# Moving loads and stores between the issue queues of SyncE, ScalarE and GpSimd in a fused attention and two-MLP kernel

## The chip, the core and the metric

The kernel runs on one core of one Trainium2 chip. The metric is the device time of one execution in microseconds (us), the median of several runs. The core's engines are TensorE (PE, with its weight loads as PEld), VectorE (DVE), ScalarE (ACT), GpSimd (POOL) and SyncE (SP). Each of SP, ACT and GpSimd can issue DMAs, each in the order of its own instructions, and each waits for semaphores before an issue; an ACT or GpSimd that waits to issue a DMA does no arithmetic meanwhile.

## The reference

Attention over chunks of 32 queries, each with 16 positions of left and 8 of right context and 8 memory positions; its output is the input x of a gated MLP, whose output is the input of a second MLP. All in float32.

```python
# q, k, v: (4, 8, 768, 64), mem_k, mem_v: (4, 8, 8, 64)
for c in range(nc):                                  # 24 chunks of 32
    k_full = concat([mem_k, k[:, :, l_start:r_end]])
    v_full = concat([mem_v, v[:, :, l_start:r_end]])
    a = softmax(scale * q_c @ k_full.T)
    out[:, :, c_start:c_end] = a @ v_full
x = out.transpose(0, 2, 1, 3).reshape(3072, 512)
y = (sigmoid(x @ w_gate) * (x @ w_val)) @ w_out      # 512 -> 1536 -> 512
h = y @ w2_in                                        # 512 -> 2048
result = (h * sigmoid(1.702 * h)) @ w2_out           # 2048 -> 512
```

## The kernel before

**Tiles and blocks.** The 3072 tokens are 32 attention tiles of 96 queries (three chunks), eight to a sequence, and six MLP blocks of 512 tokens. Tiles 0 to 5 are done in a prologue, 6 to 8 beside the first weights; tiles 9 to 31 are the late tiles, in the order 9 to 15, 30, 31, 16 to 29. Every float32 matmul is three matmuls of high and low parts.

**A late tile** (`attention` with `pe_path` False, L390). Its queries (12 DMAs) and keys (16 to 20 DMAs for two tiles) are loaded by SP (helper `dma`, issue at L350), turned by DVE (L532, L540) and multiplied on PE in one burst of 48 small matmuls (L555). The softmax runs on DVE, ACT and GpSimd, the probabilities are turned by DVE (L670), and 16 matmuls with the values (L704) run right ahead of the score burst of a later tile. The values `vn` (L676, `load_ctx`, L405: one DMA for the rows of v, one for the memory rows, one more for a tile at an edge of a sequence) have one buffer for all tiles, so a tile's load waits until the older tile's value matmuls are done. In `load_ctx` the flag `act` chooses ACT's queue; the late tiles set it.

**Where a tile's output goes** (`evict`, L720). For blocks 0 to 3 ACT and DVE cut it into high and low parts (L758, L761), the operands of the first MLP. For blocks 4 and 5 ACT copies it into `qt` (L733), the tile that a later L532 writes, and a DMA by ACT's queue (L735 to L741) stores it to `x_dram`.

**The MLPs.** Blocks 0 to 3 go through the first MLP directly (L821, L828 and L1020); its outputs are stored to `y_dram` by ACT's queue (L1044). Blocks 4 and 5 go through it in a Strassen-like form with seven products of half-sized operands (`part_product`, L1318), and so do the three pairs of blocks in the second MLP. `x_prep` (L1187) makes the operands for a pair: eight loads of 256 KB (issue at L1194, by SP) from `x_dram` or `y_dram` into the buffers `ys0` to `ys3`, differences on DVE (L1200), high and low cuts on ACT (L1178) and DVE (L1182). It is called for blocks 4 and 5 from `x_dram` (L1495), for the first pair from `y_dram` at the start of the second MLP (L1563), and for each next pair while the pair before is worked on (L1866). In the second MLP's second layer (L1655) the weights come from `wo_dram` by SP (L1611), each fetch waiting for its buffer; the weights of the products come from `wc_dram` by SP (L1225).

**The order.** A planner (`Schedule`, L34) gets every operation with an engine, a cost, what it reads and writes, and sometimes a due time. It passes due times back from users to producers, taking 2.0 us and the transfer for an SP operation and 0.2 us for one on another engine, and then fills the engines' queues in simulated time, the earliest due first among the operations that are ready. The queues' order is then fixed. A DMA costs SP or ACT 0.45 us there (0.62 for the key loads), GpSimd 1.0. Score bursts get due times of their own, 150 + 12.6 n (L601), and are held 4.5 us behind their data.

Of the kernel before, what the change touches and what calls it, by code (L numbers as in the profile page):

```python
# [18 lines left out]
P = 128  # L19
# [126 lines left out]
def kernel(  # L146
# [14 lines left out]
    nc = tc.nc  # L161
# [15 lines left out]
    BLK = 512  # L177
# [212 lines left out]
    def attention(t, bufs, banks, pe_path, extra=None, nth=0, last=False):  # L390
# [236 lines left out]
        if pe_path:  # L627

            def ev_norm(c):
                r = (c * CH, (c + 1) * CH)  # L630
                eng = nc.vector if en[c] == "dve" else nc.gpsimd
                norm(eng, T["pw"][r[0] : r[1], :, c * CH : c * CH + CTX], r, (0, CTX))

            def ev_norm_m():
                norm(nc.vector if en[0] == "dve" else nc.gpsimd, T["pw"][:, :, TK:P], (0, TQ), (CTX, KW))

            en = ["pool", "pool", "pool"] if t in (0, 2) else ["dve", "pool", "pool"]
            for c in range(NCK):
                tadd(en[c], 0.75 if en[c] == "dve" else 1.2, lambda c=c: ev_norm(c), r=ke + [kk["sm"]], w=[(kk["pw"], c)])
            tadd(en[0], 0.25 if en[0] == "dve" else 0.35, ev_norm_m, r=ke + [kk["sm"]], w=[(kk["pw"], 3)])  # L640

            def pe_pt(n):
                for h in range(H):
                    a, p = divmod(h, NP)
                    nc.tensor.transpose(  # L645
                        bt[a][:, p * TQ : p * TQ + n], T["pw"][:n, h, :], ident()[:n, :n]
                    )

            def ev_pt(a, n):
                src = bt[a][:, : NP * TQ].rearrange("p (h s) -> p h s", s=TQ)[:, :, :n]  # L650
                dst = T["pt"].rearrange("p (a h) s -> p a h s", a=2)[:, a, :, :n]
                nc.scalar.activation(dst, src, AF.Copy)

            def probs(n, more=()):
                bands = range(4) if n == TQ else (0, 3)
                r = [(kk["pw"], c) for c in bands] + [bufs.kid, *more]
                tadd("pe", 0.7 if n == TQ else 0.45, lambda: pe_pt(n), r=r, w=kbt, margin=mg)
                for a in range(2):
                    tadd("act", c_act(NP * n), lambda a=a: ev_pt(a, n), r=[kbt[a]], w=[(kk["pt"], a)])
        else:  # L660

            def ev_norm():
                norm(nc.gpsimd, T["pn"][0:L, :, 3 * CH - NM : 3 * CH], (0, L), (CTX, KW))
                norm(nc.gpsimd, T["pn"][L:TQ, :, CTX:KW], (L, TQ), (CTX, KW))

            PTB = ((0, 0, 0), (1, 0, 1), (2, 0, 2), (0, 1, 1), (1, 1, 2), (2, 1, 3), (0, 2, 3), (1, 2, 3))

            def ev_pt(part):
                for c, kb, r in PTB[2 * part : 2 * part + 2]:
                    nc.vector.transpose(  # L670
                        T["pt"][r * CH : (r + 1) * CH, :, c * CH : (c + 1) * CH],
                        T["pn"][c * CH : (c + 1) * CH, :, kb * CH : (kb + 1) * CH],
                    )

            def rest():
                load_ctx("vn", v, mem_v, True)  # L676
                tadd(
                    "pool",
                    0.95,
                    lambda: norm(nc.gpsimd, T["pn"][:, :, 0:CTX], (0, TQ), (0, CTX)),  # L680
                    r=ke + [kk["sm"]],
                    w=[(kk["pn"], 0)],
                )
                tadd("pool", 0.6, ev_norm, r=ke + [kk["sm"]], w=[(kk["pn"], 1)])
                for part in range(4):
                    tadd(
                        "dve",
                        0.88,
                        lambda part=part: ev_pt(part),
                        r=[(kk["pn"], 0), (kk["pn"], 1)],  # L690
                        w=[(kk["pt"], part)],
                    )
# [27 lines left out]
        def evict(part=None, bk=bv, kpv=kpv):  # L720

            g = range(t * NCK, (t + 1) * NCK)
            for i, blk in enumerate(sorted({c // NCH for c in g})):
                if part not in (None, i):
                    continue
                cs = [c for c in g if c // NCH == blk]
                a = (cs[0] - g[0]) * CH
                m = len(cs) * CH
                x0 = cs[0] % NCH * CH
                xb = blk % 2  # L730
                if blk >= NB - 2:
                    src, dst = values(a, m, bk), T["qt"][:, :, :m].rearrange("p (o a) s -> p o a s", o=2)
                    tadd("act", c_act(NP * m), lambda d=dst, s=src: nc.scalar.activation(d, s, AF.Copy), r=kpv, w=[kk["qt"]])  # L733
                    o = (blk - NB + 2) * BLK + x0
                    dma(  # L735
                        lambda o=o, m=m: x_dram.rearrange("(a p) c -> p a c", p=P)[:, :, o : o + m],
                        T["qt"][:, :, :m],
                        ("xd", blk, t),
                        r=[kk["qt"]],
                        act=True,  # L740
                    )  # L741
                    continue
                due = None
                if t < NPRO and blk == 0:
                    due = clock[0] - STEP * (NPRO - 1 - t) - AHEAD
                elif t < NPE and blk <= 1 and SPREAD:

                    due = clock[0] + SPREAD * (t - NPRO + 1) / (NPE - NPRO)
                src = values(a, m, bk)
                wx = [("x", xb, c % NCH, e) for c in cs for e in range(2)]  # L750
                rx = kpv + (["x1"] if xb else [])

                def at(xs, x0=x0, m=m, xb=xb):
                    dst = xs[xb][:, :, x0 : x0 + m]
                    return dst if pe_path else dst.rearrange("p (o a) s -> p o a s", o=2)

                def ev_xh(src=src, at=at):
                    nc.scalar.activation(at(xhs), src, AF.Copy)  # L758

                def ev_xl(src=src, at=at):  # L760
                    nc.vector.tensor_tensor(out=at(xls), in0=src, in1=at(xhs).bitcast(F32), op=ALU.subtract)  # L761

                tadd("act", c_act(NP * m), ev_xh, r=rx, w=wx)
                tadd("dve", c_dve(NP * m), ev_xl, r=rx, w=wx, due=due)
# [420 lines left out]
        add("pool" if pool else "dve", c_pool(BLK) if pool else c_dve(BLK), lo, r=[kst], w=[("X", m, k)])  # L1185

    def x_prep(b, mark=None, src=y_dram, b0=0, rk=lambda m, bb: [("y", m, bb)], slack=0.0):  # L1187
        for k in range(2):
            tk = 4 + k
            for i, (m, bb) in enumerate(((k, b), (k, b + 1), (2 + k, b), (2 + k, b + 1))):  # L1190

                def load(i=i, m=m, bb=bb):
                    c = slice((bb - b0) * BLK, (bb - b0 + 1) * BLK)
                    nc.sync.dma_start(out=ys[i], in_=src[m * P : (m + 1) * P, c])  # L1194

                add("sp", 0.45, load, r=rk(m, bb) + ([mark] if mark else []), w=[KYS[i]], nbytes=P * BLK * 4, slack=slack)

            def sub(o, x, y):
                def fn():
# [700 lines left out]
```

## Time and profile before

| what | us |
| --- | --- |
| median of 3 runs | 1128.76 |
| lowest and highest run | 1127.51, 1131.07 |
| the profiled execution | 1130.38 |
| its span, first to last instruction | 1128.6 |
| PE busy in the span | 1116.4 |
| DVE, ACT, POOL busy | 842.4, 589.6, 161.6 |

Issuing a DMA is not counted as busy time. A view is read for what an engine waited for: "idle 0.39 <-DMA w<-wo_dram" at a PE row says that PE stood 0.39 us before it and that the landing of that DMA ended the wait. Instants are counted from the span's first instruction.

### The profile page before, as it was taken

What the parts mean: (1) busy time and instruction counts of PE and PEld (TensorE: products, weight loads), DVE (VectorE), ACT (ScalarE), POOL (GpSimd) and SP (SyncE); (2) the same over time, 40 slices, a digit from 0 to 9 for tenths busy, and PEclk for the clock granted to TensorE, in tenths of its full rate; (3) what the DMA queues carried; (4) which work ended last, traced back from release to release, by engine and by line L of the source; (5) the groups of instructions that cost most, each with busy time, mean ns of one, the idle gap of its engine ahead of it and who ended that gap; (6) DMA issues with size and microseconds to landing.
All of it is one profiled execution on the core that took longest, in us unless ns stands there. A gap on an engine that the chain in (4) does not pass through costs nothing.

```text
span 1128.6 us, 19515 instructions
## 1 busy us (share of the span) xinstructions
PE 1116.4 (99%) x7190; PEld 933.7 (83%) x7190; DVE 842.4 (75%) x1440; ACT 589.6 (52%) x972; POOL 161.6 (14%) x209
## 2 busy tenths in 40 slices
PE   7999999999999999999999999999999999999998
PEld 6888899997888888888888888888888888888886
DVE  7989746776767788888887788869966369575365
ACT  5888632222222344676666777666455365354452
POOL 4332244122333113200001110000000000000000
PEclk9999999999999999999999999999999999999999
DMA  9676344335433555542556867868796666776526
GB/s 208 203 216 196 90 122 114 52 67 119 102 83 79 150 145 174 199 161 104 177 178 245 305 216 269 271 244 295 245 255 211 200 203 219 233 216 204 170 86 176
DMA packets 245903, 203.13 MB, mean 180 GB/s; under 512 B 170928, under 2 KB 191920, under 8 KB 245808
## 3 DMA queue, kind: packets, MB, share of 16 engines
q1 hardware_dynamic: 201560, 162.29, 48.9%
q0 software_dynamic: 6880, 24.12, 5.7%
q10 hardware_dynamic: 37368, 15.47, 5.0%
q8 instruction: 57, 0.93, 0.3%
q14 instruction: 38, 0.31, 0.1%
HBM read 151.49 MB, written 50.33 MB: 179 GB/s over the span
## 4 chain that ended last, share of the span: by engine, by line
PE 97%; DMA 1%; SPq 1%; ACT 0%; DVE 0%; issue 0%; ACTq 0%
PE bank L1318 30%; PE bank L1655 20%; PE bank L1020 18%; PE bank L821 15%; PE bank L828 8%; PE both L704 2%; PE both L555 2%; SPq L350 1%; PE bank L704 1%; PE bank L885 0%; DMA kn<-in_mem_k_dram 0%; PE bank L645 0%; DMA vn<-in_v_dram 0%; DMA w<-wo_dram 0%; PE both L645 0%
## 5 line engine op out<-in xcount | busy, mean ns | idle before, releaser
L1318 PE MATMUL bank<-sb_x,sb_r 128*128 128x512 f32 x1512 | 347.4, 389 | 0.0
L1318 PEld LDWEIGHTS bank<-sb_x,sb_r 128*128 128x128 f32 x1512 | 283.8, 188 | 58.9
L1655 PE MATMUL bank<-wq,w 128*128 128x512 f32 x756 | 178.0, 389 | 0.4 <-DMA w<-wo_dram 0.4
L1655 PEld LDWEIGHTS bank<-wq,w 128*128 128x128 f32 x756 | 141.8, 188 | 30.3 <-issue 0.8
L821 PE MATMUL bank<-xh,w 128*128 128x512 f32 (+1 forms) x464 | 159.6, 355 | 0.0
L821 PE MATMUL bank<-xl,w 128*128 128x512 f32 (+1 forms) x464 | 158.6, 353 | 0.0
L1334 DVE TENSOR_TENSOR sb_s<-bank,sb_s 128x512 f32<-128x512 f32 x108 | 74.4, 690 | 83.0 <-PE bank L1318 75.8
L828 PE MATMUL bank<-xh,w 128*128 128x512 f32 (+1 forms) x464 | 108.8, 356 | 0.0
L1020 PE MATMUL bank<-gh,wq 128*128 128x512 f32 (+1 forms) x448 | 98.7, 360 | 0.0
L821 PEld LDWEIGHTS bank<-xh,w 128*128 128x128 f32 x464 | 87.8, 189 | 12.6
L821 PEld LDWEIGHTS bank<-xl,w 128*128 128x128 f32 x464 | 87.8, 189 | 11.9
L1330 ACT ACTIVATE sb_s<-bank 128x512 f32<-128x512 f32 x108 | 64.8, 604 | 50.7 <-PE bank L1318 49.9
L828 PEld LDWEIGHTS bank<-xh,w 128*128 128x128 f32 x464 | 78.1, 189 | 12.4
L1020 PEld LDWEIGHTS bank<-gh,wq 128*128 128x128 f32 x448 | 76.4, 189 | 12.9
L670 DVE STREAM_TRANSPOSE pt<-raw 32x256 f32<-32x256 f32 x184 | 79.5, 432 | 4.7 <-POOL raw L623 2.1
L1626 DVE TENSOR_TENSOR wq<-xh_g,wq 128x1024 fp32r<-128x1024 f32 (+1 forms) x60 | 60.5, 1008 | 22.9 <-ACT wq L1623 22.5
L1623 ACT ACTIVATE wq<-xh_g 128x1024 fp32r<-128x1024 f32 (+1 forms) x60 | 53.3, 889 | 35.2 <-PE bank L1655 34.2
L853 ACT ACTIVATE gh<-sig 128x512 fp32r<-128x512 f32 (+1 forms) x58 | 32.3, 557 | 67.4 <-DVE sig L848 61.6
L623 POOL TENSOR_TENSOR raw<-e,sm 96x448 f32<-96x448 f32 (+2 forms) x69 | 41.0, 606 | 176.1 <-DVE sm L615 149.0
L1655 PE MATMUL bank<-wq,w_e 128*128 128x512 f32 x252 | 62.5, 389 | 0.0
L845 ACT ACTIVATE sig<-bank 128x512 f32<-128x512 f32 (+1 forms) x58 | 30.5, 526 | 55.5 <-PE bank L828 49.7
L1655 PEld LDWEIGHTS bank<-wq,w_e 128*128 128x128 f32 x252 | 47.3, 188 | 9.8
(215 smaller groups left out, 1646.1 us busy)
## 6 DMA issues: line engine op xcount, KB each, us to landing
sb_r<-wc_dram SPq DMA_DIRECT2D x133, 256.0 KB
w<-wo_dram SPq DMA_DIRECT2D x63, 512.0 KB
w_e<-wo_dram SPq DMA_DIRECT2D x21, 512.0 KB
wc_dram<-sb_r SPq DMA_DIRECT2D x15, 512.0 KB
wo_dram<-w POOLq DMA_DIRECT2D x14, 512.0 KB, 3.9
raw<-in_moe_w_out_dram SPq DMA_DIRECT2D x13, 512.0 KB
raw<-in_moe_w_in_dram SPq DMA_DIRECT2D x13, 512.0 KB
wf_dram<-f POOLq DMA_DIRECT2D x24, 256.0 KB, 2.9
```

The costliest lines, as they stand in the source:

```text
L623: eng.tensor_tensor(out=dst, in0=e3()[r, :, c], in1=T["sm"][r].to_broadcast([n, H, keys[1] - keys[0]]), op=ALU.mult)
L670: nc.vector.transpose(T["pt"][r * CH : (r + 1) * CH, :, c * CH : (c + 1) * CH], T["pn"][c * CH : (c + 1) * CH, :, kb * CH : (kb + 1) * CH],)
L704: nc.tensor.matmul((bk if to is None else to)[hp * D : (hp + 1) * D, o : o + q], T["vn"][:, 2 * p + hp, :], T["pt"][:, hp * NP + p, :q], s ...
L821: nc.tensor.matmul(bank[bk][:, :n], w[:, 0, ts[t]], x[xb][:, t, c0 : c0 + n], start=t == 0 and x is xhs, stop=False)
L828: nc.tensor.matmul(bank[bk][:, :n], w[:, 1, ts[t]], xhs[xb][:, t, c0 : c0 + n], start=False, stop=t == NK - 1)
L1020: nc.tensor.matmul(bank[into[m]][:, c0 : c0 + n], w[:, wi, m * P : (m + 1) * P], g[:, :n], start=f == 0 and j == 0 and c0 == 0, stop=f == ...
L1318: nc.tensor.matmul(bank[bk], w[:, o : o + P], xt[x, k][:, xl, :], start=first and k == 0 and wl == 0 and xl == 0, stop=k == 1 and wl == 1, ...
L1330: add("act", c_act(BLK), lambda: nc.scalar.activation(work[n], bank[bk], AF.Copy), r=[("bank", bk)], w=[n])
L1334: nc.vector.tensor_tensor(out=work[n], in0=bank[bk], in1=work[n], op=ALU.add)
L1623: nc.scalar.activation(quad[b_][:, c, 0, :], src(js), AF.Copy)
L1626: nc.vector.tensor_tensor(out=quad[b_][:, c, 1, :], in0=src(js), in1=quad[b_][:, c, 0, :].bitcast(F32), op=ALU.subtract)
L1655: nc.tensor.matmul(bank[bk], lhs, quad[b_][:, x, gl_, :], start=begin, stop=last and x == js[-1] and wl == 1, skip_group_check=not first,)
```

## The change

Three edits. The late tiles' value loads are issued by SP instead of ACT. The late tiles' x stores to `x_dram` are issued by SP instead of ACT. In `x_prep`, the loads for the second and the third pair of blocks in the second MLP (the calls with b = 2 and b = 4 from `y_dram`) are issued by GpSimd at a planned cost of 1.0 instead of by SP at 0.45; the calls from `x_dram` and for the first pair stay on SP. The planner takes each operation on its new engine, so that the order of the queues can change with it. The first MLP's output stores are on ACT's queue before and after.

```diff
             def rest():
-                load_ctx("vn", v, mem_v, True)
+                load_ctx("vn", v, mem_v)
                 tadd(
...
                         T["qt"][:, :, :m],
                         ("xd", blk, t),
                         r=[kk["qt"]],
-                        act=True,
                     )
...
     def x_prep(b, mark=None, src=y_dram, b0=0, rk=lambda m, bb: [("y", m, bb)], slack=0.0):
+        side = 0 < b < NB - 2 or b and src is y_dram
         for k in range(2):
...
-                    nc.sync.dma_start(out=ys[i], in_=src[m * P : (m + 1) * P, c])
-
-                add("sp", 0.45, load, r=rk(m, bb) + ([mark] if mark else []), w=[KYS[i]], nbytes=P * BLK * 4, slack=slack)
+                    (nc.gpsimd if side else nc.sync).dma_start(out=ys[i], in_=src[m * P : (m + 1) * P, c])
+
+                add("pool" if side else "sp", 1.0 if side else 0.45, load, r=rk(m, bb) + ([mark] if mark else []), w=[KYS[i]], nbytes=P * BLK * 4, slack=slack)
```

## Rows read from the trace of the kernel before

**Rows 1.** The page, part 1: busy us (share of the span) x instructions, by engine
```profile
PE 1116.4 (99%) x7190; PEld 933.7 (83%) x7190; DVE 842.4 (75%) x1440; ACT 589.6 (52%) x972; POOL 161.6 (14%) x209
```
**Rows 2.** The page, part 4: shares of the chain that ended last, by engine
```profile
PE 97%; DMA 1%; SPq 1%; ACT 0%; DVE 0%; issue 0%; ACTq 0%
```
**Rows 3.** Stretches: length, busy PE, PEld, DVE, ACT, POOL (x), clock, DMA share, GB/s
```profile
0.00:20.00 20.00, 14.00 (x296) 12.09 (x301) 13.67 (x24) 10.58 (x22) 7.84 (x14) 1.00 0.95 183
250.00:300.00 50.00, 49.14 (x434) 39.44 (x436) 34.77 (x75) 13.43 (x26) 15.15 (x22) 1.00 0.50 113
1087.00:1128.60 41.60, 36.84 (x166) 30.06 (x164) 27.39 (x36) 12.57 (x15) 0.00 (x0) 0.98 0.60 177
```
**Rows 4.** Timeline of PE, 784 to 796: start, us, instruction, [idle before <-releaser]
```profile
793.19 3.00 PE L1655 MATMUL bank<-wq,w 128*128 128x512 f32 x12 [0.39 <-DMA w<-wo_dram]
```
**Rows 5.** The chain that ended last, 260 to 300: start, us, what
```profile
273.34 0.68 PE both L555 x46
...
275.60 4.50 DMA vn<-in_v_dram
...
280.13 0.28 ACTq L350
...
282.11 4.17 PE bank L1020 x17
```
**Rows 6.** Waits of ACT, 139 to 480: total us, times, longest
```profile
ACT xh L758 <- PE both L555: 28.3, 13, 4.6
...
ACT kt L544 <- DMA vn<-in_mem_v_dram: 9.2, 2, 5.0
...
ACT kt L544 <- DMA f<-in_q_dram: 6.2, 2, 3.8
```
**Rows 7.** Line L350, all DMA issues: ns min/median/max, first and last start
```profile
L350 ACTq DMA_DIRECT2D vn<-in_v_dram x28: 279/332/635, 142.5 to 450.7; - x28
...
L350 ACTq DMA_DIRECT2D vn<-in_mem_v_dram x23: 278/353/1044, 145.2 to 451.2; - x23
...
L350 ACTq DMA_DIRECT2D x_dram<-qt x12: 377/420/1043, 274.6 to 459.6; - x12
```
**Rows 8.** Timeline of SP, 139 to 480
```profile
256.81 11.29 SPq L350 DMA_DIRECT2D f<-in_q_dram  x24
268.14 8.70 SPq L350 DMA_DIRECT2D raw<-in_k_dram  x16
```
**Rows 9.** Timeline of DVE, 262 to 275
```profile
265.59 0.56 DVE L532 STREAM_TRANSPOSE qt<-f 128x384 f32<-128x384 f32 x1
```
**Rows 10.** Timeline of ACT, 455 to 500
```profile
459.64 0.39 ACTq L350 DMA_DIRECT2D x_dram<-qt  x1
```
**Rows 11.** Timeline of SP, 415 to 480
```profile
463.81 11.80 SPq L1194 DMA_DIRECT2D xh_y<-x_dram  x6
```
**Rows 12.** Timeline of DVE, 480 to 491
```profile
483.24 0.68 DVE L1182 TENSOR_TENSOR sb_x<-xl_y,sb_x 128x512 fp32r<-128x512 f32 x1
```
**Rows 13.** Timeline of PE, 480 to 491
```profile
482.56 8.32 PE L1318 MATMUL bank<-sb_x,sb_r 128*128 128x512 f32 x36
```
**Rows 14.** Timeline of SP, 735 to 822
```profile
787.29 0.32 SPq L1194 DMA_DIRECT2D sb_y<-y_dram  x1
788.76 0.32 SPq L1611 DMA_DIRECT2D w<-wo_dram  x1
```
**Rows 15.** Line L1432, GpSimd's stores of 512 KB: ns min/median/max, first and last start
```profile
L1432 POOL DMA_DIRECT2D wo_dram<-w x14: 710/727/780, 417.9 to 666.4; - x14
```
**Rows 16.** Timeline of DVE, 755 to 830
```profile
814.83 0.68 DVE L1182 TENSOR_TENSOR sb_x<-sb_y,sb_x 128x512 fp32r<-128x512 f32 x1
```
**Rows 17.** Timeline of PE, 816 to 820
```profile
817.79 2.43 PE L1318 MATMUL bank<-sb_x,sb_r 128*128 128x512 f32 x10
```
**Rows 18.** Timeline of DVE, 244 to 262
```profile
260.05 0.54 DVE L761 TENSOR_TENSOR xl<-both,xh 128x384 fp32r<-128x384 f32 x1
```
**Rows 19.** Timeline of PE, 252 to 268
```profile
260.56 0.39 PE L821 MATMUL bank<-xh,w 128*128 128x512 f32 x1
```

## The prediction

> **What bounds the kernel now.** I read the page's busy line first: TensorE (PE) is busy 1116.4 of 1128.6 us [rows 1]. The chain that ended last then says whether that is work or pipelined waiting: 97% of it is PE, DMA 1%, SyncE's queue 1% [rows 2]. The windows show where the missing 12.2 us lie: 6.0 in the first 20 us, 4.76 in the last 41.6, 0.86 between 250 and 300 [rows 3]; another 0.39 precedes one matmul at 793.19 [rows 4], and 0.2 is left over. In all these stretches the granted clock is 0.98 to 1.00, the upper of the two levels (2.4 GHz). The head and the tail come from the first tiles' loads and the last block, which the change does not touch. So the change has at most 0.86 + 0.39 = 1.25 us to win (0.11%), unless it makes PE do other work, which it does not. What it can lose has no such limit: PE runs its instructions in the written order, and each one whose operand is late stops it.
>
> The 0.86 us is the case that the change aims at. Read the chain backwards [rows 5]: PE goes on at 282.11, after ScalarE (ACT) had issued a value load at 280.13, which itself stood until the load of 275.60 had landed 4.50 us later. ACT's evictions queue behind its own DMA issue. The waits of ACT say the same in sum: 9.2 us before one line on the landing of memory values, and 6.2 us on query loads that SyncE (SP) had issued and that this line does not read [rows 6]. I read that as DMAs of both queues taking turns on a few completion semaphores: a new one waits until an older one has landed.
>
> **Part 1, late tiles' values to SP.** 28 value loads and 23 loads of memory values leave ACT for SP, at 332 and 353 ns (medians) [rows 7]: 28 x 0.332 + 23 x 0.353 = 17.4 us of issue time, 2.2 issues per tile over 23 tiles. On ACT it costs nothing to take them away, since ACT is not the bound, and it gives back the 0.86. On SP they are added to a queue that has no idle time there: 24 query loads take 11.29 us from 256.81, and the next group begins at 268.14 [rows 8]; twenty such rows abut from 139.51 to 291.3, never 0.4 us apart. Each tile brings a wait too: SP now stands until the older tile's value matmuls have freed the one buffer, and for tiles at a sequence's edge until the first part has landed. Queued behind that are the query and key loads of the next tiles, for which VectorE's (DVE) transposes and then PE's score burst wait.
>
> How much cover is there? The tightest place that I find is the tile of the burst at 273.34 [rows 5]. Its twelve query loads are the first half of the 24, so issued by 256.81 + 11.29/2 = 262.5; a landing after 2.3 us is an estimate, half of the 4.50 us that a value load of fifteen times their size took [rows 5]. So they land near 264.8, and their transpose begins at 265.59 and takes 0.56 [rows 9]: 0.8 us of cover there and 273.3 - 266.2 = 7.1 us from there to the burst, 7.9 in all. Against it stand eight tiles' issues, 8 x 2.2 x 0.34 = 6.0 us, and one edge tile, whose third part stands until the first has landed (4.5 us, 275.60 to 280.13). 10.5 - 7.9 = 2.6 us late at most, if SP has not a single gap and the order of its queue stays. The hand-made planner knows SP's issue costs (0.45 and 0.62) and keeps bursts 4.5 us away from their data in its own time, so it will move bursts rather than let PE meet a late one. I take 0; bounds 0 (PE has nothing more to win there) and +2.6.
>
> **Part 2, x stores to SP.** 12 issues of 420 ns (5.0 us) leave ACT for SP [rows 7]. Eleven free the tile that a later query transpose writes, and such a transpose begins some 7 us ahead of its burst [rows 5, 9], so a store that is 0.7 us later (a value pair ahead of it) costs nothing. The last is delicate: issued at 459.64, read back by the loads of 463.81 [rows 10, 11], from which the second MLP's operands are cut. DVE ends the second product's operand at 483.24 + 0.68 = 483.92 [rows 12], and that product begins with the seventh matmul from 482.56 on, at 227 ns each (8.32 us for 36, the last one's 0.39 included), so at 482.56 + 6 x 0.227 = 483.92 [rows 13]. Cover: nothing. An SP that is free issues the store as soon as ACT does now, 0 us; a value pair queued ahead costs 0.33 + 0.35 = 0.7. I take 0; bounds 0 and 0.7.
>
> **Part 3, the pair's loads to GpSimd's queue.** 16 loads in two groups of eight leave SP. Does a weight fetch wait behind them? At 787.29 SP issues such a load (0.32), then stands 1.15 us and fetches at 788.76 [rows 14]; so the fetch waited for something else (its buffer), and the load ahead of it was no hindrance. The 0.39 us at PE [rows 4] is that fetch's landing. Taking 0.25 MB from in front of it could shorten it: between 0 and 0.39, and I take 0, since both transfers still run at once. GpSimd has been idle there, its issues of 0.5 MB stores took 727 ns (780 at most) [rows 15], and the last operand of the group is ready at 814.83 + 0.68 = 815.5, for the sixth product of a sequence that begins at 817.79 [rows 16, 17], so 5 x 1.36 = 6.8 us later (six matmuls of 0.227 each): 9 us of cover hide a slower issue.
> The Trainium skill (SBUF — State Buffer, "Who interferes with whom") warns that descriptors of GpSimd-issued DMAs are written through a port that DVE can lock in its two-port modes, so that such a DMA waits for DVE. The rows on issue times above don't show it (727 ns median, 780 at most, in a span of which DVE is busy 75% [rows 1]), though none of them lies in the second MLP.
>
> **The sum.** -0.86 + 0 + 0 = -0.86 us. The profiled execution took 1130.38 (its span 1128.6 and 1.8 around it), 1.62 above the median of the runs, which is within their spread (1127.51 to 1131.07); I subtract from the median: 1128.76 - 0.86 = 1127.9.
>
> **Rivals.** (A) SP becomes the bound, the one that ends slower. Place: 139 to 290, where SP's groups abut [rows 8]. Mechanism: SP meets the value load before PE has freed the buffer and stands, and all query and key loads behind it slip. ACT, which makes the same wait today by its eviction, stood 28.3 us in 13 such places, 2.2 each [rows 6]. If SP stands so at none to two of the eight tiles, PE loses the 2.6 from above and up to 4.4 more. It decides from the point where the loads slip by more than 7.9 us. A second gate makes it worse: DVE cuts the last x of block 2 at 260.05 + 0.54 = 260.59, and PE's first products on that block begin at 260.56 [rows 18, 19]; a burst that slips there is paid in full. Price 2.6 to 7.0 us, time 1130.5 to 1134.9, middle 1132.7. For it: no idle SP. Against it: a queue that is late itself does not arrive early at a wait.
> The Trainium skill (Perfetto Trace Analysis, "What "DMA-bound" means" and "DMA Optimizations") counts an issuing engine whose track is solid DMA as a bound of its own, and advises to spread DMAs over the issuing engines; by that rule part 1 goes the wrong way, and the time would be that of this rival. The SP rows agree that the track is solid; that PE waits for it they don't show.
> (B) The x stores come late: part 2's gate with no cover. SP standing at another load (a 3 us wait as at an edge tile) delays all operands of the second MLP's first products: 1127.9 + 1 to 3 = 1129 to 1131.
> (C) GpSimd issues late, against part 3: only what exceeds 9 us of cover counts, 0 to 4 us: 1128 to 1132.
> (D) The moved waits don't vanish: x and value loads still share completion semaphores with ACT's y stores, so ACT stands there instead, and the 0.86 stays: 1128.8.
> (E) The planner finds another, better order: the idle left outside head and tail is 1.25 us, so more than 0.3% (3.4 us, about what a measurement here tells from no change) would have to come from head or tail. I see no way to it.
>
> **How the numbers follow.** Forecast (-1.25 to +0.5 us, 1127.5 to 1129.3): 0.50. D: 0.12. B: 0.08. A: 0.24. C: 0.03. E: 0.03. Within 0.3% (1125.4 to 1132.1) lie the forecast, D, B, half of C and a third of A: 0.50 + 0.12 + 0.08 + 0.015 + 0.08 = 0.795, given as 0.79. Slower: the rest of A and C, 0.18. Faster: 0.03. The range starts at the fastest run less the most to win, 1127.5 - 1.25 = 1126.3, given as 1126, and reaches to 1133, the middle of A; outside stay half of A, E and a little of C, under 0.2.
>
> **What would show it.** Right: no PE idle at 282 and no ACT wait on value landings; PE's idle total 11 to 12 us, all in head and tail; L1194 on GpSimd's queue with X ready before 818. Wrong: new idle before a score burst between 160 and 300, released by a transpose that waits for query loads (A); idle between 480 and 495 before L1318 (B) or after 818 (C); ACT standing at L1044's stores (D). If PE's busy time itself moves by over 1 us, the argument from idle time has failed.

## The result, and the profile after

The changed kernel takes 1136.43 us (1133.64 to 1137.34, six runs) beside 1128.74 (1127.51 to 1131.07, six runs): the ratio is 1.0064, 95% interval 1.0049 to 1.0079. It is 7.7 us slower, and above the predicted range (1126 to 1133). The profiled execution took 1136.34 us, its span is 1134.4: 5.96 and 5.8 more than before. The traces can place these 5.8 us. The rest of the 7.7 no trace places: the profiled execution of the kernel before lies 1.64 us above its median.

The page of the changed kernel, busy line and shares of the chain that ended last:

```profile
PE 1120.6 (99%) x7190; PEld 937.4 (83%) x7190; DVE 841.6 (74%) x1440; ACT 588.7 (52%) x972; POOL 168.0 (15%) x225
...
PE 77%; SPq 15%; DMA 3%; issue 2%; DVE 1%; ACT 0%; DVEq 0%; ACTq 0%
```

Beside [rows 1] and [rows 2]: PE's busy time grew by 4.2 us over the same 7190 matmuls (what of it is which is told below), and SyncE's queue, 1% of the chain before, is 15% of it now. Three stretches of the changed kernel (columns as in [rows 3]):

```profile
250.00:300.00 50.00, 49.49 (x448) 40.12 (x446) 36.08 (x75) 13.77 (x26) 14.99 (x20) 1.00 0.47 109
400.00:450.00 50.00, 45.95 (x364) 36.99 (x362) 37.78 (x79) 22.48 (x37) 12.84 (x20) 0.93 0.54 138
1093.00:1134.40 41.40, 37.17 (x167) 30.36 (x165) 27.71 (x36) 12.90 (x15) 0.00 (x0) 0.97 0.60 178
```

Before the change PE was busy for all of 400 to 450, at clock 1.00. Now 4.05 us are idle there and the mean granted clock is 0.93. From the waits of PE after the change (total us, times, longest), the largest, and the only other one at this line:

```profile
PE both L704 <- DMA vn<-in_mem_v_dram: 4.0, 1, 4.0
...
PE both L704 <- DVE sm L612: 0.5, 1, 0.5
```

From L741 on, the changed kernel's lines have one number less than before (L1019 is L1020 of before). PE's timeline after the change, and below it the same instructions before it:

```profile
285.49 0.88 PE L704 MATMUL both<-pt,vn 128*64 128x96 f32 x16
...
391.31 0.88 PE L704 MATMUL both<-pt,vn 128*64 128x96 f32 x16
...
401.76 0.39 PE L820 MATMUL bank<-xl,w 128*128 128x512 f32 x1
406.20 1.55 PE L704 MATMUL both<-pt,vn 128*64 128x96 f32 x16 [4.05 <-DMA vn<-in_mem_v_dram]
407.68 1.09 PE L555 MATMUL both<-kt,qt 64*32 64x64 f32 x48
408.70 2.07 PE L827 MATMUL bank<-xh,w 128*128 128x512 f32 x4
...
412.90 1.07 PE L827 MATMUL bank<-xh,w 128*128 128x512 f32 x4
413.80 1.98 PE L1019 MATMUL bank<-gh,wq 128*128 128x512 f32 x8
```
```profile
286.21 0.88 PE L704 MATMUL both<-pt,vn 128*64 128x96 f32 x16
...
391.39 0.88 PE L704 MATMUL both<-pt,vn 128*64 128x96 f32 x16
...
402.15 0.88 PE L704 MATMUL both<-pt,vn 128*64 128x96 f32 x16
...
407.39 1.98 PE L1020 MATMUL bank<-gh,wq 128*128 128x512 f32 x8
```

PE's order hardly changed: 6866 of its 7190 matmuls have the same names and shapes at the same place in both kernels. So subtract the starts of the same instruction, and the loss has a place. At the value matmuls of 286 the changed kernel is 0.72 us ahead: the 0.86 us idle at 282 [rows 5] are gone. At 391 it is 0.08 ahead (a new 0.5 us wait for a softmax step took most of it back). At the next value matmuls it is 4.05 behind, and at the gate's output matmuls 6.41 behind. So one wait costs 4.13, and 2.36 more go by 413.8 without any idle time: four matmuls take 2.07 us at 408.70 and 1.07 at 412.90. The granted clock in between, from the windows of the changed kernel (length, busy PE, clock, DMA share, GB/s):

```profile
404.80:411.60 6.80, 5.40 (x71) 0.50 0.37 67
```

0.50 is the lower of the clock's two levels (1.2 GHz). Up to 1060 us the same instructions stay 6.3 to 6.4 us behind; the last stretch then has 4.23 us of idle time (41.40 - 37.17) in place of 4.76 [rows 3].

Why was the value load late? SyncE's timeline after the change:

```profile
384.50 0.48 SPq L350 DMA_DIRECT2D vn<-in_v_dram  x1
385.08 0.63 SPq L350 DMA_DIRECT2D x_dram<-qt  x1
...
386.70 3.70 SPq L350 DMA_DIRECT2D raw<-in_k_dram  x4
390.47 11.74 SPq L350 DMA_DIRECT2D f<-in_q_dram  x22
402.31 0.89 SPq L350 DMA_DIRECT2D vn<-in_v_dram  x2
403.30 0.38 SPq L350 DMA_DIRECT2D x_dram<-qt  x1
403.73 0.41 SPq L350 DMA_DIRECT2D vn<-in_mem_v_dram  x1
```

The value buffer came free when the value matmuls of 391.31 ended, at 392.19. The load for the next tile (tile 24, the first of its sequence, so in three parts) went out at 402.31, 10.1 us later, behind 22 query loads; its memory part at 403.73 landed 2.33 us later in the chain, and PE went on at 406.20. Before the change ScalarE issued the same three parts from right behind the eviction on (ScalarE's timeline before):

```profile
392.97 0.49 ACT L733 ACTIVATE qt<-both 128x384 f32<-128x384 f32 x1 [3.14 <-PE both L555]
393.50 0.34 ACTq L350 DMA_DIRECT2D vn<-in_v_dram  x1
...
397.15 0.30 ACTq L350 DMA_DIRECT2D vn<-in_mem_v_dram  x1
397.50 0.33 ACTq L350 DMA_DIRECT2D vn<-in_v_dram  x1
```

The first part is 1.2 us after the buffer was free. The last two are 4.9 and 5.2 us after it, since ScalarE stood for landings in between, and even so they were in time for 402.15. Measured so for each late tile but the first, the changed kernel's value loads are 0 to 2.5 us late up to 236, 3.4 to 10.5 between 250 and 430 (10.1 and 10.5 are the two loads of rows of tile 24), and on time again from 437 on. SyncE runs behind its plan from 250 to 430, and one view says whether it does: when SyncE is ahead, it stands until DVE's query transpose (L532) has freed a buffer for the next query loads. The waits of SyncE, 139 to 480, before the change have that line; after it no such line exists:

```profile
SPq L350 <- DVE qt L532: 9.6, 5, 3.2
```

Of these 9.6 us, 9.4 lie between 371 and 411; earlier SyncE stands for a query transpose once, for 0.24 us. So the queue that the prediction found without idle time up to 291 had its room only at the end of the query loads.

The largest waits of SyncE from 139 to 420 after the change:

```profile
SPq L350 <- DMA y_dram<-f: 5.1, 4, 2.0
SPq L350 <- PE both L704: 1.7, 2, 1.1
```

SyncE hardly stands for the value buffer (1.7 us). It stands 5.1 us for the landing of y stores that ScalarE issued and that its own loads do not read. The prediction read such stands as DMAs of both queues taking turns on completion semaphores. The traces bear it out, as they name for each DMA the semaphore that its landing counts up. In every run here the DMAs of SyncE and ScalarE use the same eight, GpSimd's another eight, and each of these four stands is for the semaphore that SyncE's own load uses next and that a y store used last.

### The profile page after: what moved, and what is told of

It is laid out like the page before. It is cut to its first block, busy times and chain, and to the rows that moved or that the text cites. A ratio compares the mean times of both kernels' runs of the same rounds, so it can differ in the third digit from the quotient of the medians.

```text
span 1134.4 us, 19539 instructions
## 1 busy us (share of the span) xinstructions
PE 1120.6 (99%) x7190; PEld 937.4 (83%) x7190; DVE 841.6 (74%) x1440; ACT 588.7 (52%) x972; POOL 168.0 (15%) x225
## 4 chain that ended last, share of the span: by engine, by line
PE 77%; SPq 15%; DMA 3%; issue 2%; DVE 1%; ACT 0%; DVEq 0%; ACTq 0%
PE bank L1318 30%; PE bank L1655 20%; SPq L350 15%; PE bank L1019 12%; PE bank L820 8%; PE bank L827 4%; DMA f<-in_q_dram 1%; PE both L704 1%; DMA y_dram<-f 1%; DMA raw<-in_moe_w_val_dram 1%; PE both L555 1%; DVE pt L670 1%; DMA qn<-in_q_dram 1%; DMA w<-wo_dram 0%; PE bank L704 0%
## 5 line engine op out<-in xcount | busy, mean ns | idle before, releaser
L1019 PE MATMUL bank<-gh,wq 128*128 128x512 f32 (+1 forms) x448 | 98.9, 361 | 0.0
L827 PEld LDWEIGHTS bank<-xh,w 128*128 128x128 f32 x464 | 78.6, 190 | 12.5 <-issue 0.2
L1019 PEld LDWEIGHTS bank<-gh,wq 128*128 128x128 f32 x448 | 76.4, 189 | 13.1
L623 POOL TENSOR_TENSOR raw<-e,sm 96x448 f32<-96x448 f32 (+2 forms) x69 | 38.2, 564 | 184.5 <-DVE sm L615 153.3
```

What stands on the lines that cost most here:

```text
L623: eng.tensor_tensor(out=dst, in0=e3()[r, :, c], in1=T["sm"][r].to_broadcast([n, H, keys[1] - keys[0]]), op=ALU.mult)
L827: nc.tensor.matmul(bank[bk][:, :n], w[:, 1, ts[t]], xhs[xb][:, t, c0 : c0 + n], start=False, stop=t == NK - 1)
L1019: nc.tensor.matmul(bank[into[m]][:, c0 : c0 + n], w[:, wi, m * P : (m + 1) * P], g[:, :n], start=f == 0 and j == 0 and c0 == 0, stop=f == ...
```

## The experiments

All are compared with runs of the kernel before on the same chip. "Stands" is SyncE's wait for the query transpose (us, times) from 139 to 480, "last load" the start of its last query load in the profiled execution, "more" the number of DMAs that it issues at line L350 beyond those of the kernel before.

| run | us | ratio, 95% interval | stands | last load | more |
| --- | --- | --- | --- | --- | --- |
| before | 1128.74 | | 9.6, 5 | 415.9 | |
| the change | 1136.43 | 1.0064 [1.0049, 1.0079] | none | 429.3 | 63 |
| e1 part 1 alone | 1136.56 | 1.0063 [1.0047, 1.0079] | none | 425.5 | 51 |
| e2 part 2 alone | 1129.03 | 0.9993 [0.9983, 1.0003] | 12.5, 5 | 414.1 | 12 |
| e3 part 3 alone | 1130.33 | 1.0004 [0.9992, 1.0015] | 11.6, 5 | 415.5 | 0 |
| e11 parts 2 and 3 | 1130.15 | 1.0009 [1.0000, 1.0018] | 14.7, 6 | 414.5 | 12 |
| e4 change, one tile on ScalarE | 1137.41 | 1.0070 [1.0052, 1.0088] | none | 428.6 | 60 |
| e5 change, planned price 0.50 | 1141.34 | 1.0090 [1.0065, 1.0114] | none | 439.2 | 63 |
| e6 change, 2 of 12 query loads by ScalarE | 1147.36 | 1.0154 [1.0139, 1.0169] | 4.3, 3 | 431.1 | 17 |
| e7 before, 2 idle loads per tile | 1138.85 | 1.0088 [1.0072, 1.0104] | 0.5, 1 | 423.7 | 46 |
| e8 before, values by GpSimd | 1136.30 | 1.0057 [1.0042, 1.0072] | 13.5, 6 | 414.7 | 12 |
| e9 change, 2 of 12 query loads by GpSimd | 1133.88 | 1.0039 [1.0023, 1.0056] | 7.0, 5 | 419.3 | 17 |
| e9b change, 4 of 12 by GpSimd | 1131.01 | 1.0010 [0.9999, 1.0021] | 18.5, 9 | 414.3 | -29 |
| e10 before, odd tiles' values on SyncE | 1142.29 | 1.0115 [1.0097, 1.0134] | 0.8, 2 | 429.8 | 27 |
| e12 before, even tiles' values on SyncE | 1135.35 | 1.0052 [1.0035, 1.0069] | 2.8, 1 | 423.1 | 24 |
| e13 before, 4 of 12 query loads by GpSimd | 1128.81 | 0.9995 [0.9986, 1.0005] | 30.2, 13 | 411.5 | -92 |

(Runs of the kernel before beside them had medians of 1129.72 for e1 to e4, 1129.49 for e5 to e8, 1129.59 for e9 to e11, 1129.68 for e12 and e13.)

Every kernel in which SyncE issues 17 DMAs or more beyond those of before loses time, 4.3 to 17.9 us. Of those with 12 or fewer only e8 does, and there the wait hangs on a load of GpSimd's. The size of the loss does not follow the number: the planner orders each of these kernels anew, so each time is that of its edit and of the order that comes with it.

**Which part: e1, e2, e3, e11.** Each of the first three makes one edit of the change to the kernel before; e11 undoes the first edit in the changed kernel.

```diff
 e1:
-                load_ctx("vn", v, mem_v, True)
+                load_ctx("vn", v, mem_v)
 e2:
-                        act=True,
 e11, against the changed kernel:
-                load_ctx("vn", v, mem_v)
+                load_ctx("vn", v, mem_v, True)
```

> Part 1 alone: the late tiles' values by SP, the x stores left on ACT, the pair's loads left on SP. Theory T (the value loads stand in SP's queue behind query loads that SP issues later than planned, so one value product of the tile after the second sequence edge finds no values): a stall of 2 to 4 us at a value product near 402, and 2 to 2.5 us of halved clock behind it, so 1132 to 1136. Rival R1 (the x stores, which make SP wait for ScalarE, are what puts SP behind): no stall over 0.9 us, 1127.5 to 1129. Rival R2 (the pair's loads by GpSimd): 1127.5 to 1129 as well, with the value loads still late by up to 10 us after the buffer is free.

> Part 2 alone: the x stores by SP, values left on ACT. T: the value loads go out within 1 to 2 us after their buffer is free, no stall at 402, 1128 to 1130. R1: SP stands at the stores, a stall of 2 us or more somewhere between 270 and 410, 1131 to 1135. The gate at the second MLP's first products (no cover) would show as idle of up to 3 us near 483.

> Part 3 alone: the next pair's loads by GpSimd, the rest as before. T: 1128.4 to 1128.9, the 0.86 us at 282 still there. R2: 1131 to 1135, with idle behind 765.

> The changed kernel with part 1 undone: late tiles' values on ScalarE again, x stores on SyncE and the pair's loads on GpSimd as in the change. If the loss is part 1 alone and the other two parts don't act on one another: as e2 and e3, 1127.5 to 1130.5, and the 0.86 us idle at 282 us as absent as in e2. If the parts work together (SyncE's stores with GpSimd's loads): 1132 or more.

Part 1 alone gives the whole loss, 6.84 us, with the same wait at the same instant, longer than theory T had it (waits of PE in e1, 139 to 480):

```profile
PE both L704 <- DMA vn<-in_mem_v_dram: 5.6, 2, 5.4
```

Parts 2 and 3, alone or together, are within 0.3% of before. In e2 the 0.86 us at 282 is absent and nothing new stands at 483; in e3 it is still there (0.95), and its time, though level with before, lies above the 1128.4 to 1128.9 that I expected. Each of the three traces has one wait of PE of 1.3 to 1.4 us near 450 that the trace of before lacks; the times don't show it.

**One load, or the whole queue: e4.** The changed kernel, but the value load of tile 24, the one that came late at 402, is issued by ScalarE again.

```diff
-                load_ctx("vn", v, mem_v)
+                load_ctx("vn", v, mem_v, t == 24)
```

> The whole change, but the value loads of the one tile whose product stood 4.05 us (the first of the third sequence) stay on ACT's queue. T: that stall and the halved clock behind it are gone (4.05 + 2.35 us), 1129.5 to 1131; the other value loads are still late by 5 to 9 us without a cost. Rival R3 (SP as a whole is too late, the stall only moves to another tile's product or transpose): a stall of 2 us or more elsewhere before 460, 1133 to 1137.

The wait did not go; it passed to the next operand of the same burst, and the time (1137.41) is the top of rival R3's. PE's timeline of e4:

```profile
407.92 1.09 PE L555 MATMUL both<-kt,qt 64*32 64x64 f32 x48 [5.38 <-DVE qt L532]
```

Now the scores wait for a query transpose, whose loads SyncE issued late. So it is not the place of one load in the order that costs, as I had thought, but SyncE's lateness as a whole.

**The planner's price: e5.** 24 query loads take 11.29 us [rows 8], 0.47 each, where the planner reckons 0.45. Here it is told 0.50.

```diff
                             r=pre,
+                            dur=0.5,
```

> The whole change, with one number of the planner altered: a late tile's query load is planned at 0.50 us of SP instead of 0.45 (measured 0.47 to 0.50 each in SP's abutting rows). Theory T2 (SP runs behind its plan because its issues are dearer than planned; PE's order is planned for loads that land earlier): the planner moves bursts behind their loads, no stall over 1 us near 402 to 410, 1128 to 1131. Rival R4 (SP has more work than it can do, whatever the plan says): a stall of 2 us or more before 460, 1132 to 1138.

It loses more, 11.9 us, which is beyond rival R4's 1138 too. The planner's order spreads the lateness over other bursts (waits of 2.0 before 260.8, 2.9 before 435.2, 2.2 before 462.3). A better price does not give SyncE time that it does not have.

**Issues without any wait: e7.** The kernel before, with two more 16 KB loads per late tile on SyncE into a buffer that nothing reads. They wait for no PE and replace nothing.

```diff
+            for x in range(2):
+                z = CH * (nth % 2 * 2 + x)
+                dma(
+                    lambda z=z: pad0[z : z + CH, : NP * CH].rearrange("p (a r) -> p a r", r=CH),
+                    q[b].rearrange("(p two) s d -> two s p d", two=2)[0][j * TQ : j * TQ + CH, :, x * CH : (x + 1) * CH],
+                    ("pad", z),
+                    r=pre,
+                )
```

> The kernel before, with two more loads of 16 KB per late tile on SP, into a tile that nothing reads: 46 issues with nothing to wait for. N: SP runs behind as in the change, a late query transpose makes a score burst wait 3 to 6 us near 403, with the halved clock 1132 to 1137. W: SP stays on time, 1128.5 to 1130.5.

9.4 us slower, though values, stores and pair loads are where they were before, and 1.9 us beyond what N gave. The costliest wait is for a sigmoid at 390 and not, as N had it, for a query transpose near 403. PE's timeline of e7, then SyncE's, then DVE's:

```profile
390.23 0.79 PE L830 MATMUL bank<-xh,w 128*128 128x512 f32 x1 [2.81 <-ACT sig L854]
```
```profile
375.63 1.87 SPq L350 DMA_DIRECT2D pad<-in_q_dram  x4
377.61 0.39 SPq L292 DMA_DIRECT2D xl_y<-in_moe_w_in_dram  x1
```
```profile
381.47 0.43 DVE L301 TENSOR_SCALAR xl_y<-xl_y 128x512 int32<-128x512 int32 x1 [6.71 <-DMA xl_y<-in_moe_w_in_dram]
```

A weight load of SyncE's went out behind the idle loads at 377.61 (370.75 before); DVE stood 6.71 us for it and ScalarE 6.8, and the sigmoid came late behind them. So the number of issues on SyncE is enough to cause the loss; that a moved load waits for value matmuls is not needed.

**Relief by ScalarE: e6.** The changed kernel with two of twelve query loads per late tile on ScalarE's queue.

```diff
                             r=pre,
+                            act=r == 0 and c < 2,
```

> The whole change, but two of the twelve query loads of each late tile go to ACT's queue: 46 issues leave SP, 51 came to it. Theory N (the number of issues on SP is what puts it behind): the value loads go out within 4 us after their buffer is free, no stall over 1 us, 1127.5 to 1130. Rival W (SP falls behind because it stands at the value loads until the buffer is free, and at x stores): the value loads stay late by 6 to 10 us and a stall of 2 us or more stays, 1132 to 1138.

The worst of all, 17.9 us, beyond what either theory gave. SyncE has 17 issues more than before the change, where the change has 63, and yet it stands. Its two longest waits from 139 to 480, and PE's worst row in e6:

```profile
SPq L350 <- DMA f<-in_q_dram: 24.0, 23, 2.8
SPq L350 <- PE both L705: 17.1, 4, 6.9
```
```profile
266.74 0.80 PE L821 MATMUL bank<-xl,w 128*128 128x512 f32 x1 [4.57 <-DVE xl L761]
```

23 waits for query loads that have nothing to do with the waiting load. By the semaphores, 21.0 us of them, up to 420, are for one that a query load of ScalarE's used last; 10.8 us more are for one that a y store of ScalarE's used. Relief on a queue with which SyncE takes turns is none. That row is also the second gate that the prediction named (block 2's last x).

**Values by GpSimd: e8.** The kernel before, with the late tiles' value loads by GpSimd (the large part in two halves) and the x stores on SyncE.

```diff
+            parts = [(a, z, s, slice(0, H)) for a, z, s in parts]
+            if pool:
+                a, z, s, _ = parts[0]
+                parts[:1] = [(a, z, s[x : x + H // 2], slice(x, x + H // 2)) for x in (0, H // 2)]
...
-                load_ctx("vn", v, mem_v, True)
+                load_ctx("vn", v, mem_v, pool=True)
```

> The kernel before, with the late tiles' value loads on GpSimd's queue (the large part in two halves of four heads) and the x stores on SP; the pair's loads stay on SP. N and W alike: SP is relieved of nothing but gets only 12 issues, ACT is free of the value loads, GpSimd has room: no stall over 1 us, the 0.86 us at 282 gone, 1127.5 to 1129. Rival G (GpSimd's products of the softmax wait behind the value loads, and probabilities come late): idle of 1 us or more before a value product, 1130 to 1134.

SyncE keeps its room (13.5 us of stands), and the loss, 6.8 us, beyond what either theory gave, has another cause. GpSimd's timeline in e8, and PE's wait:

```profile
442.39 0.81 POOL L350 DMA_DIRECT2D vn<-in_v_dram  x1 [0.22 <-issue]
447.69 0.79 POOL L350 DMA_DIRECT2D vn<-in_v_dram  x1 [4.49 <-issue]
```
```profile
450.72 0.88 PE L708 MATMUL both<-pt,vn 128*64 128x96 f32 x16 [2.60 <-DMA vn<-in_mem_v_dram]
```

The second half went out 5.3 us after the first, and the view names no releaser ("issue"). The landings tell what it waited for: the first half landed at 447.34, 0.35 us ahead. In 20 of the 23 late tiles the second half goes out 0.32 to 0.37 us after the first has landed, though that takes 2.7 to 5.0 us from the issue; in the other three, the last tile of a sequence each, it goes out at once. So two halves of a value load don't queue behind one another here as SyncE's loads do. Why GpSimd waits for the landing no run here shows.

**Relief by GpSimd: e9, e9b, e13.** e9 is e6 with the queue exchanged: the same two query loads per tile, by GpSimd at a planned 1.0. e9b moves four; e13 moves the same four in the kernel before.

```diff
 e9:
                             r=pre,
+                            pool=r == 0 and c < 2,
+                            dur=1.0 if r == 0 and c < 2 else 0.45,
 e9b, and e13 against the kernel before:
                             r=pre,
+                            pool=r == 0 or c == 0 and r == 64,
+                            dur=1.0 if r == 0 or c == 0 and r == 64 else 0.45,
```

> The changed kernel, with two of a late tile's twelve query loads issued by GpSimd (planned at 1.0) and ten by SyncE. SyncE issues about 46 fewer, as many as before the change. The edit is that of e6 with another queue. Theory S (what costs is SyncE's time: its own issues and its stands for DMAs of ScalarE with which it takes turns; GpSimd's loads take no turns with them): the value loads go out within 3 us of their buffer being free, no wait of PE before the value matmuls nor before the scores over 1 us, granted clock at its upper level until the last block, 1127.5 to 1131. Theory G (any DMA that comes late by GpSimd replaces the loss, since its issue is slow or its planned cost makes the planner move bursts): PE waits 2 to 5 us before a score burst for a query transpose, 1133 to 1139. Theory V (the value load on SyncE is late by its place in the planned order, whatever else SyncE has to do): value loads 6 to 10 us late as after the change, 1134 to 1138.

> As the run before, with four of the twelve query loads by GpSimd. Theory S: no later than with two, SyncE issues some 440 between 139 and 420 us, value loads on time, 1127.5 to 1131. Theory G: the loss grows with the number of loads on GpSimd, 1136 to 1145. Theory V: as after the change, 1134 to 1138.

> The kernel before, with four of a late tile's twelve query loads issued by GpSimd and nothing else changed: the relief of e9b without the change. If the relief only gives SyncE room and the kernel before had enough of it: 1127.5 to 1131, SyncE stands more than 15 us for query transposes. If GpSimd's loads bring a cost of their own (which would stand in e9b's time as well): over 1131, with PE waiting for a query transpose. If SyncE's lack of room costs the kernel before too: under 1127; the 0.86 us idle at 282 us are all that its trace offers.

With two loads the loss falls from 7.7 to 4.3 us, with four to 1.4, which the interval does not tell from none. With two, SyncE still issues 17 more than before the change (the expectation left out the 12 x stores), with four 29 fewer. With two, theory S's time (up to 1131) was missed: value loads were still up to 8.8 us late near 295, and PE waited for one. With four its time holds but for a hair (1131.01), though not its 3 us for every value load: an edge tile's was 7.6 us late at 398 and cost the one wait of PE left there. SyncE stands 18.5 us for query transposes again. Theories G and V fall: more loads on GpSimd cost less, and the value load is late only while SyncE has too much to do. PE's timeline of e9; then the waits of PE, and those of SyncE, from 139 to 480 in e9b:

```profile
298.06 1.14 PE L706 MATMUL both<-pt,vn 128*64 128x96 f32 x16 [2.08 <-DMA vn<-in_v_dram]
```
```profile
PE both L706 <- DMA vn<-in_mem_v_dram: 1.0, 1, 1.0
```
```profile
SPq L350 <- DVE qt L534: 18.5, 9, 3.3
```

e13 has more room still (30.2 us of stands) and is level with before: the relief has no cost that shows and, with SyncE not short of time, no gain.

**Half of the values: e10, e12.** The kernel before with only the odd (e10) or only the even (e12) late tiles' values on SyncE.

```diff
 e10:
-                load_ctx("vn", v, mem_v, True)
+                load_ctx("vn", v, mem_v, t % 2 == 0)
 e12:
-                load_ctx("vn", v, mem_v, True)
+                load_ctx("vn", v, mem_v, t % 2 == 1)
```

> The kernel before, with the value loads of the odd late tiles alone on SyncE; the even tiles' stay on ScalarE, stores and pair loads are as before. Some 25 issues more on SyncE instead of 51. A queue that fills up (theory S): half the issues fit into the stands that SyncE has before the change (some 20 us in the stretch against 25 x 0.43 = 11 us), value loads late by at most 4 us, loss 0 to 2 us, 1128.5 to 1131. A cost for each value load on SyncE (theory V): half of the loss of the changed kernel, 3 to 5 us, 1132 to 1134.

> The mirror of e10: the kernel before with the value loads of the even late tiles alone on SyncE. Theory S (SyncE has no room in this stretch; what is late is whatever stands next in its queue, so that the size of the loss depends on the planner's order): SyncE hardly ever stands for a query transpose any more (under 2 us in all, 9.6 before the change), the last query load goes out after 420 us, PE waits somewhere between 200 and 480 for an operand that hangs on a SyncE load, loss 2 to 13 us, 1131 to 1142; the place is another than in e10. Theory O (odd tiles are special: three of them are the edge tiles with a third load that waits for the first): the even tiles cost at most 2 us, 1128.5 to 1131.5.

I had expected that half of them fits. It does not: e10 loses 12.7 us, more than all of them do and than either theory gave, and e12 5.7. In e10 the victim is neither a value nor a query. DVE's timeline of e10, then SyncE's, then PE's:

```profile
388.19 0.43 DVE L301 TENSOR_SCALAR xl_y<-xl_y 128x512 int32<-128x512 int32 x1 [9.84 <-DMA xl_y<-in_moe_w_in_dram]
```
```profile
378.92 5.33 SPq L350 DMA_DIRECT2D raw<-in_k_dram  x11
384.34 0.39 SPq L292 DMA_DIRECT2D xl_y<-in_moe_w_in_dram  x1
```
```profile
391.10 0.79 PE L821 MATMUL bank<-xh,w 128*128 128x512 f32 x1 [3.44 <-DVE sig L848]
```

A weight load queued behind key loads went out at 384.34; DVE, whose order is fixed, stood 9.84 us at the instruction that reads it, and the first MLP's sigmoid product queued behind (DVE's row at 390.40 comes after it) stopped PE for 3.44 us. Here SyncE also stands for value loads of ScalarE (22.7 us in nine waits, 3.9 in four before the change): with values on both queues they take turns more often. In e12 the longest wait is 2.15 us, for a value at 379.87, then 1.90 for a sigmoid at 393.19. Behind that sigmoid is the weight load of e7 and e10 once more: issued at 381.40, with DVE standing 8.88 us for it. So e12's place near 390 is that of e10, against what I had expected, and SyncE stands a little longer for query transposes than I gave it (2.8 us, under 2 expected). That SyncE has no room holds in both, and the odd tiles are nothing special; how much is lost depends on what stands next in the queue. What makes e10 dearer than the whole of part 1 I can point at (the weight load, the turns) but did not separate.

## Why the prediction was wrong

**The bound** was read rightly: PE's idle time was 12.2 us, and at most 1.25 could be won. It was won for a moment: at 286 the changed kernel is ahead by 0.72, with no idle time at 282, and ScalarE's waits for DMA landings at L544, both lines of [rows 6], are gone. Rival D (the moved waits stay) falls. But the prediction named a busy time that moves by over 1 us as the sign that arguing from idle time has failed, and it moved by 4.2: 2.36 of it at the lower clock, 0.33 in the last stretch (37.17 against 36.84), and 1.5 in the first 40 us (35.29 against 33.77), which leave PE only 0.4 us behind there and have no consequence. Time lost without idling was in none of its terms.

**Part 1, the step that failed**, is the zero: "The hand-made planner ... keeps bursts 4.5 us away from their data in its own time, so it will move bursts rather than let PE meet a late one. I take 0". Its own time was the trouble. In the real one SyncE fell behind by up to 10 us, and 4.5 us of distance do not cover that. I had written that SyncE has no idle time there [rows 8] and then let a plan that assumes such time pay the bill.

Two terms under it were mis-sized. The cover was worked out at one burst (273.34, 7.9 us) and for query loads alone. The value load has cover too, and I did not work it out: at 392 the buffer came free at 392.19, the next value matmuls stood at 402.15 before the change, and the issue of its three parts, with an x store between them, and the last landing took 403.73 + 2.33 - 402.31 = 3.75 us, so 402.15 - 392.19 - 3.75 = 6.2 us. It was 10.1 us late: 3.9 too much, close to the 4.13 measured. And the issue time was too low. The late tiles' value loads after the change (columns as in [rows 7]):

```profile
L350 SPq DMA_DIRECT2D vn<-in_v_dram x28: 278/385/581, 160.1 to 459.8; - x28
L350 SPq DMA_DIRECT2D vn<-in_mem_v_dram x23: 306/443/567, 166.7 to 460.2; - x23
```

Added up, the 51 issues took 20.3 us on SyncE, and on ScalarE before they had taken 19.1: the median times the number, 17.4, was low already there. That is 3 us more in the queue than I reckoned.

**Rival A** had the mechanism (SyncE becomes the bound) at 0.24, and one of its victims: query and key loads, which slipped in e4. Its place, 139 to 290, was too early: lateness grows from 250 on and PE meets it at 402. Its step "SP meets the value load before PE has freed the buffer and stands" is the wrong way round: up to 420 SyncE stood 1.7 us for that, and the value load was itself late behind query loads. The argument against A, that a late queue does not arrive early at a wait, was true and should have been read as the cause. Its price, 2.6 to 7.0 us on top of the 0.86 won, takes in the wait of 4.13; 2.36 us at the lower clock came to that, and no more than 0.08 was left of the gain.
The rule of the Trainium skill that stood beside A (Perfetto Trace Analysis, "What "DMA-bound" means": a sequencer track of solid DMA slices is a bound) agrees with e7, where two idle loads per tile cost 9.4 us. Its advice for that case ("DMA Optimizations": balance DMAs over the engines that can issue them) holds in e9 and not in e6: with the same two loads per tile the changed kernel loses 4.3 us if GpSimd issues them and 17.9 if ScalarE does.

**Part 2** was right at 0: e2 is level with before, and the products that read x begin 6.4 us later than before (488.99 after the change, 482.56 before [rows 13]), the lag that PE already had, and PE has no wait between 425 and 1085 but the 0.4 us for a weight of [rows 4]. Rival B falls. **Part 3** was right at 0: e3 is level, and rival C falls; GpSimd's issues of 256 KB took 538 ns each (16, at most 554), less than the 727 that I took. Rival E found nothing.

**The chances**: slower got 0.18 with half of A left outside the range. Its price should have had no upper end at a single tile's lateness: every tile of 23 adds 2.2 issues to a queue that does not catch up until 430.

No version here beats the kernel before: e2 (0.9993) and e13 (0.9995) are level with it, as idle time of 1.25 us would have it.

## What to carry to other kernels

Before work is moved to an issue queue, look for the waits that show that it runs ahead (here, stands for a buffer that its consumer frees): a queue with 9.6 us of these in 340 us had no room for 20 us of issues, nor for half of them, and the loss falls on whatever operand stands next in it. Work out the cover of the moved load itself, not only of those behind it. Relief has to come from a queue that does not make the first one wait for its landings.

## What was unexpected of the hardware

A wait of PE can cost more than its length. In the 4.05 us before 406.20 the granted clock fell to 0.50, at 404.8, and stood there for 6.8 us, and the matmuls in it came 2.36 us late. In e10 it stood at 0.50 from 390.5 to 393.9 after 3.44 us idle, in e7 for 3.4 us after 2.81 idle. The length of the last wait alone does not tell: in e12 the clock stayed up after 2.15 us idle at 379.87, and fell after 1.90 at 393.19.

A longer issue is no loss where the queue has room: GpSimd issued query loads of 16 KB in 554 ns (median of 92 in e9b, at most 723; 430 on SyncE) with no wait of PE behind them. The same late value loads took 20.3 us to issue on SyncE and 19.1 on ScalarE, the x stores 5.0 and 5.8, so the issue time itself hardly depends on which of the two issues.
